# Joining chunk 4's scores to the sums of values: one group of four banks in a fused attention and expert kernel

## The chip, the cores and the metric

The kernel runs on one core of a Trainium2 chip. The time is the device time of one execution in microseconds (us). The kernel before took 1122.79 us in the median of three runs (1121.68, 1122.79 and 1124.22).

## What is computed

The reference is block-causal attention followed by a two-layer expert with a sigmoid gate, all in float32:

```python
batch, n_heads, seq, head_dim = (8, 8, 576, 64)
scores = scale * np.matmul(q, k.transpose(0, 1, 3, 2))
scores = np.where(block_i >= block_j, scores, -1000000000.0)   # blocks of 64
attn = np.exp(scores - np.max(scores, axis=-1, keepdims=True))
attn = attn / (np.sum(attn, axis=-1, keepdims=True) + 1e-09)
x = np.matmul(attn, v)            # to (4608, 512), heads side by side
...
h = x @ w_in                      # 512 to 2048
g = h * (1.0 / (1.0 + np.exp(-1.702 * h)))
return g @ w_out                  # 2048 to 512
```

## The kernel before

**Turns.** Heads go in pairs, 32 pairs, one pair a turn (`step(n)`, n from 0). The 576 queries of a head are cut into five chunks: chunk 0 has 64 queries, chunks 1 to 4 have 128, and chunk i sees 64 (2i + 1) keys, so chunk 4 sees all 576. The two heads of a pair lie on partitions 0 to 63 and 64 to 127, and their score matmuls (64 partitions each) run side by side on TensorE. An order of a turn is written out by hand in `ORDER`: each word is a slot, `3+0/2+1` scores chunks 3 and 0 in one pair of banks and 2 and 1 in another, `4` chunk 4, `V` the sums of values of the pair before (`av(n - 1)`), `L` the transposes of the next pair's queries and keys (`prep`). Between the slots the expert's matmuls are let in.

**Scores (`score`, `weigh`, `normalise`, `turn`).** For each chunk TensorE writes the scores into PSUM banks, `bank`. The vector engine adds the mask, scales and takes the row minimum in one instruction (L351, with an accumulator read for the maximum `mx`), ScalarE takes the exponential with a row sum (L358), the vector engine makes a scalar of the sum (L368, L371), and GpSimd (L376) or the vector engine (L378) scales the rows, as `SCALE_ON` says: "P" GpSimd, "D" the vector engine. From the ninth turn on (n of 8 and more) the vector engine turns the weights in 32x32 blocks (L385, L390), and behind chunk 4 sixteen DMAs on SP's queue put the blocks into their places (`turned<-turned`), where the next turn's sums of values read them. Before that TensorE turns them (`flip`). The tile of weights `e` has two buffers, one for chunks 0, 2 and 4, one for 1 and 3. Chunk 4's 576 keys do not fit a bank of 512: its scores are cut at 256, and take four banks.

**Banks.** `bank()` hands out tiles in a fixed round; from the tenth turn on there are four, w0 to w3. A tile can be written when the one before it in the same bank has been read.

**The expert.** Tokens go in 12 tiles of 384, the hidden layer in 16 chunks of 128 per tile. A hidden chunk is 12 matmuls into `hp` (one bank), then tanh on ScalarE (L562), the product `g` on the vector engine (L563), a high part `gh` on ScalarE (L571) and a low part `gl` on GpSimd (L82); the second layer is 9 matmuls into `acc` for the hidden chunk before. `hp` of the next hidden chunk can begin when `g` of this one has read the bank. So TensorE's list from the tenth turn on is a row of hp and acc, with a group of attention matmuls behind some hp. Six or so hidden chunks pass in a turn.

**What sets the order.** TensorE's matmuls stay in the order in which the program writes them (`keep_in_program_order`); on the other engines a scheduler at build time places the instructions, from the program's order and priorities (`tc.high_priority` for tanh, g, gh, gl and the tiles' splits xh and xl). Each engine then works off its list in order, and an instruction that waits holds up all behind it.

Of the kernel before, what the change touches and what calls it, by code (L numbers as in the profile page):

```python
# [10 lines left out]
F32 = mybir.dt.float32  # L11
# [5 lines left out]

SCALE_ON = ("PPPPP", "PPPPP", "PPPPD")  # L20

# [4 lines left out]
ORDER = (  # L26
# [3 lines left out]
)  # L30

START = "1+0 - B 2/3 L C - V - 4 - a - - -"
# [8 lines left out]
def attention_moe_kernel(  # L41
# [9 lines left out]
    nc = tc.nc  # L51
# [52 lines left out]

    ident = sp.tile([P, P], F32, name="ident")
    make_identity(nc, ident)
    MW = 448
    mask = sp.tile([P, MW], mybir.dt.bfloat16, name="mask")
    nc.gpsimd.memset(mask, 0.0)
    nc.gpsimd.memset(mask[0:BLK, MW - BLK : MW], -8e9)  # L110
# [16 lines left out]
        return home[name, g]  # L127

    xr = sp.tile([P, NDC, RING], F32, name="xr")


    vp = sp.tile([P, 2, NCH, D], F32, name="vp")
# [159 lines left out]
    def prep(n):  # L292

        tag = "e0" if early(n) and n % 2 else "qk"
        qk[n] = d2.tile([P, 2, S], F32, tag=tag, name="qk", bufs=1)
        for x in range(2):
            nc.vector.transpose(out=qk[n][:, x], in_=raw[n][:, x].rearrange("p c d -> p (c d)"))  # L297
        raw.pop(n)
        m = follower(n)
        if m is not None:  # L300
            load(m)

    stats = {}

    def score(n, banks):

        if n not in stats:
            mx = d2.tile([P, NCH + 1, 2], F32, tag="mx", name="mx")
            sm = d2.tile([P, NCH, 2], F32, tag="sm", name="sm")
            stats[n] = (mx, sm)  # L310
        todo = []
        for chunks in banks:

            part = []
            for lo, hi in ((0, 512),) if width(chunks[0]) <= 512 else ((0, 256), (256, S)):
                ss = [bank() for _ in range(2)]
                c = 0
                for i in chunks:
                    a, z = qrange(i)
                    w = min(hi, width(i)) - lo  # L320
                    for hd in range(2):
                        r = slice(hd * D, hd * D + D)

                        mm(
                            out=ss[hd][:, c : c + w], lhsT=qk[n][r, 0, a : a + P],
                            rhs=qk[n][r, 1, lo : lo + w], start=True, stop=True,
                        )
                        part.append((i, hd, lo, lo + w, ss[hd][0 : z - a, c : c + w]))
                    c += w
            todo.append(sorted(part, key=lambda x: (chunks[::-1].index(x[0]), x[2])))  # L330
        for chunks, part in zip(banks, todo):
            e = {}
            for i, hd, lo, hi, s in part:
# [30 lines left out]
    def normalise(n, i, e):  # L364
        _, sm = stats[n]
        m = BLK if i == 0 else P
        c = sm[0:m, i]
        nc.vector.tensor_scalar(  # L368
            out=c, in0=c, scalar1=1e-9, scalar2=2.0, op0=ALU.add, op1=ALU.mult
        )  # L370
        nc.vector.reciprocal(out=c, in_=c)  # L371
        on = SCALE_ON[phase(n)][i]
        for hd in range(2):
            x, sc = e[0:m, hd], c[:, hd : hd + 1]
            if on == "P":
                nc.gpsimd.tensor_tensor(out=x, in0=x, in1=sc.to_broadcast([m, width(i)]), op=ALU.mult)  # L376
            elif on == "D":
                nc.vector.tensor_scalar(out=x, in0=x, scalar1=sc, scalar2=None, op0=ALU.mult)  # L378
            else:
                nc.scalar.activation(out=x, in_=x, func=AF.Copy, scale=sc)  # L380

    def turn(n, i, e):

        for hd in range(2 if i else 0):
            nc.vector.transpose(  # L385
                out=tw[:, :, SLOT[i] : SLOT[i] + i, hd].rearrange("p b j c -> p j b c"),
                in_=e[:, hd, 0 : i * P],
            )
        r = slice(BLK, P) if i else slice(0, BLK)
        nc.vector.transpose(  # L390
            out=tw[r, 0:2, 9 + max(i, 1)].rearrange("p b h c -> p h b c"), in_=e[r, :, i * P : width(i)]
        )
        if i == NCH - 1:
            for kb in range(4):
                for qb in range(4):
                    ns = 10 if kb > 1 else NS if qb > 1 else 11
                    nc.sync.dma_start(
                        out=pw[kb * 32 : kb * 32 + 32, qb, 0:ns], in_=tw[qb * 32 : qb * 32 + 32, kb, 0:ns]
                    )
# [26 lines left out]
                in_=src[:, x : x + 2 * len(part), a : a + 2],  # L426
            )

    def av(n):

        b, h = divmod(n, HP)
        before_av(n)
        o, o0 = bank(), bank()

        todo = []
        for i in range(1, NCH):
            c = (i - 1) * P
            todo += [(o, c, P, j, pw[:, :, SLOT[i] + j]) for j in range(i)]
            todo.append((o, c + BLK, BLK, i, pw[:, 2:4, 9 + i]))
        last = len(todo) - 1  # L440
        todo.append((o0, 0, BLK, 0, pw[:, 0:2, 10]))

        for x, (bk, c, nn, j, w) in enumerate(todo):
            for hd in range(2):
                mm(
                    out=bk[hd * D : hd * D + D, c : c + nn].rearrange("d (a c) -> d a c", c=32),
                    lhsT=values(n)[:, hd, j], rhs=w[:, :, hd], start=x in (0, last + 1), stop=x >= last,
                )
# [12 lines left out]
    def order(n):  # L461
        return {HP: START, 2 * HP: HANDOVER}.get(n, ORDER[phase(n)]).split()

    def step(n):
# [112 lines left out]
        yield from second(prev)  # L577


    ends = np.cumsum([0.0] + [NFC * chunk_time(tt) for _, tt in TILES])  # L580

    def quota(pos):
        xs, ys = zip(*TILES_BY)
        return -1.0 if pos < xs[0] else np.interp(pos, xs, [ends[y if y >= 0 else y - 1] for y in ys])

    def heads_for(t):
        return -(-sum(TILES[t]) // S) * H
# [36 lines left out]
    for n in range(NPAIR + 1):  # L624
        items = step(n)
        for sl, fn in enumerate(items):
            if fn is not None:
                fn()
            if order(n)[sl] == "V":
# [35 lines left out]
```

## Time and profile before

| | |
|---|---|
| median of three runs | 1122.79 us |
| profiled execution, own time | 1120.49 us |
| its span, first to last instruction | 1118.6 us |
| mean granted TensorE clock | 0.992 of full speed |
| TensorE busy | 1076.4 us (96%) |
| vector engine busy (DVE) | 583.0 us (52%) |
| ScalarE busy (ACT) | 498.6 us (45%) |
| GpSimd busy (POOL) | 406.7 us (36%) |

The profile was taken by the hardware in one execution. A row of its timeline has the start and the duration in us, the engine, the line of the program, the operation, the tiles written and read (`out<-in`), the shape, a count where equal rows follow each other, and in brackets the idle time before it with what ended it. Matmuls are pipelined, and the duration of one reaches past the start of the next: what a matmul costs is read from start to start. A float32 matmul shows as two rows.

### The profile page before, as it was taken

The page shows a single profiled execution, that of the slowest core. Times are in us where ns is not written, and L with a number is a line of the kernel's source. Part 1 is how long each engine was busy: PE and PEld are TensorE (multiplying, and loading weights), DVE is VectorE, ACT ScalarE, POOL GpSimd, SP SyncE. Part 2 cuts the span into 40 slices and gives each one's busy share as a digit, 9 for nine tenths or more (in the row PEclk, how much of TensorE's full clock was granted, in tenths as well). Part 3 has the DMA queues.
Part 4 walks back from the last instruction along what each step waited for, and adds up shares of the span by engine and source line. Part 5 has one row for each costly group of instructions (what it writes and reads, how often), then busy time and mean ns, then how long its engine had stood idle before and what let it go on. Part 6 is the DMA issues. An engine that isn't in the chain of part 4 may idle for free. (4 is left out here: it accounts for less than half of the span.)

```text
span 1118.6 us, 19977 instructions
## 1 busy us (share of the span) xinstructions
PE 1076.4 (96%) x6960; PEld 908.7 (81%) x6960; DVE 583.0 (52%) x1856; ACT 498.6 (45%) x1321; POOL 406.7 (36%) x509
## 2 busy tenths in 40 slices
PE   5969998999999999999999999999999999999998
PEld 3757776788888888888888888888888888899997
DVE  6776885545545555654555655645545654211210
ACT  5866776434534433534443543444434444322322
POOL 4665664333333332333333333333333233122222
PEclk9979999999999999999999999999999999999999
DMA  8734532332444432343443333344342332200000
GB/s 171 205 89 153 150 73 62 84 79 57 105 86 86 103 80 64 64 98 78 98 101 74 75 93 65 70 108 85 81 107 63 71 85 58 54 29 1 29 1 29
DMA packets 219365, 91.25 MB, mean 82 GB/s; under 512 B 197760, under 2 KB 197760, under 8 KB 219264
## 3 DMA queue, kind: packets, MB, share of 16 engines
q1 hardware_dynamic: 214528, 89.38, 34.0%
q10 hardware_dynamic: 4736, 0.59, 0.3%
q8 instruction: 55, 0.90, 0.3%
q14 instruction: 46, 0.38, 0.1%
HBM read 45.09 MB, written 9.44 MB: 49 GB/s over the span
## 5 line engine op out<-in xcount | busy, mean ns | idle before, releaser
L82 POOL TENSOR_TENSOR gl<-g,gh 128x384 fp32r<-128x384 f32 x192 | 194.7, 1014 | 551.5 <-ACT gh L571 449.1
L99 PE MATMUL hp<-xh,wih 128*128 128x384 f32 x768 | 264.7, 345 | 7.9 <-DVE g L563 6.9
L563 DVE SCALAR_TENSOR_TENSOR g<-g,hp 128x384 f32<-128x384 f32 x192 | 105.9, 552 | 319.1 <-ACT g L562 317.8
L99 PE MATMUL hp<-xh,wil 128*128 128x384 f32 x768 | 258.4, 336 | 0.1
L562 ACT ACTIVATE g<-hp 128x384 f32<-128x384 f32 x192 | 94.1, 490 | 359.8 <-PE hp L99 354.8
L99 PE MATMUL hp<-xl,wih 128*128 128x384 f32 x768 | 253.9, 338 | 0.4 <-DVE xl L82 0.4
L99 PE MATMUL acc<-woh,gh 128*128 128x512 f32 x576 | 233.9, 406 | 0.0
L99 PE MATMUL acc<-wol,gh 128*128 128x512 f32 x576 | 226.9, 394 | 0.0
L99 PEld LDWEIGHTS hp<-xh,wih 128*128 128x128 f32 x768 | 144.2, 188 | 34.1 <-DVE g L563 23.1
L99 PE MATMUL acc<-woh,gl 128*128 128x512 f32 x576 | 167.9, 393 | 0.3 <-POOL gl L82 0.3
L571 ACT CAST gh<-g 128x384 fp32r<-128x384 f32 x192 | 98.4, 513 | 156.5 <-DVE g L563 156.4
L99 PEld LDWEIGHTS hp<-xh,wil 128*128 128x128 f32 x768 | 144.3, 188 | 6.5 <-POOL wil L82 0.7
L358 ACT ACTIVATE e<-e,mx 64x64 f32<-64x64 f32 (+4 forms) x240 | 132.3, 552 | 37.6 <-DVE mx L351 37.6
L376 POOL TENSOR_TENSOR e<-e,sm 64x64 f32<-64x64 f32 (+1 forms) x192 | 113.6, 612 | 95.0 <-DVE sm L371 46.5
L99 PEld LDWEIGHTS hp<-xl,wih 128*128 128x128 f32 x768 | 143.6, 188 | 1.3 <-DVE xl L82 1.3
L99 PE MATMUL bank<-qk 64*128 64x320 f32 (+4 forms) x768 | 122.5, 428 | 14.5 <-DVE qk L297 11.1
L99 PEld LDWEIGHTS acc<-woh,gh 128*128 128x128 f32 x576 | 107.9, 187 | 34.2 <-issue 10.5
L99 PEld LDWEIGHTS acc<-woh,gl 128*128 128x128 f32 x576 | 107.8, 188 | 25.9 <-POOL gl L82 1.2
L99 PEld LDWEIGHTS acc<-wol,gh 128*128 128x128 f32 x576 | 108.3, 188 | 16.7 <-POOL wol L82 0.3
L351 DVE CUSTOM_DVE_ANT_0 e<-bank,mask 64x64 f32<-64x64 f32 (+4 forms) x240 | 89.7, 417 | 56.9 <-PE bank L99 52.8
L385 DVE STREAM_TRANSPOSE turned<-e 128x384 f32<-128x384 f32 (+1 forms) x192 | 92.3, 499 | 48.8 <-POOL e L376 48.3
L99 PEld LDWEIGHTS bank<-qk 64*128 64x128 f32 x768 | 69.6, 193 | 54.2 <-issue 25.4
(50 smaller groups left out, 956.0 us busy)
## 6 DMA issues: line engine op xcount, KB each, us to landing
turned<-turned SPq DMA_DIRECT2D x192, 80.0 KB, 2.1
turned<-turned SPq DMA_DIRECT2D x96, 112.0 KB, 2.2
raw<-in_q_dram SPq DMA_DIRECT2D x128, 72.0 KB, 2.4
out_dram<-osb SPq DMA_DIRECT2D x36, 256.0 KB, 2.2
raw<-in_k_dram SPq DMA_DIRECT2D x120, 72.0 KB, 2.6
turned<-turned SPq DMA_DIRECT2D x96, 88.0 KB, 2.1
words<-in_moe_w_in_dram SPq DMA_DIRECT2D x16, 512.0 KB, 6.3
vp<-in_v_dram SPq DMA_DIRECT2D x60, 128.0 KB, 2.4
```

Of the source, the lines that this page charges most:

```text
L82: eng.tensor_tensor(out=out, in0=in0, in1=in1, op=ALU.subtract)
L99: return tc.keep_in_program_order(nc.tensor.matmul(**kw))
L351: nc.vector.tensor_tensor_reduce(out=e[0:m, hd, lo:hi], in0=s, in1=mk, op0=ALU.add, op1=ALU.min, scale=-0.125, scalar=3e38 if lo == 0 else ...
L358: nc.scalar.activation(out=e[0:m, hd], in_=e[0:m, hd], func=AF.Exp, scale=-1.0, bias=mx[0:m, i, hd : hd + 1], accum_out=sm[0:m, i, hd : hd ...
L376: nc.gpsimd.tensor_tensor(out=x, in0=x, in1=sc.to_broadcast([m, width(i)]), op=ALU.mult)
L385: nc.vector.transpose(out=tw[:, :, SLOT[i] : SLOT[i] + i, hd].rearrange("p b j c -> p j b c"), in_=e[:, hd, 0 : i * P],)
L562: nc.scalar.activation(out=g, in_=hp[:, 0:tt], func=AF.Tanh, scale=1.702)
L563: nc.vector.scalar_tensor_tensor(out=g, in0=g, scalar=1.0, in1=hp[:, 0:tt], op0=ALU.add, op1=ALU.mult)
L571: nc.scalar.copy(out=gh, in_=g)
```

## The change

From the tenth turn on (n of 9 and more) the slot `V4` takes the place of `V` and `4`. It takes a bank `o0`, runs the sums of values of the pair before, and scores chunk 4 of this pair directly behind. Chunk 4's first 512 keys of each head go into a bank of their own; the last 64 keys of both heads are one matmul of 128 partitions against a tile `ends`, in which the two heads' keys stand on the diagonal with zeros beside them, and their scores lie in the unused part of `o0`. So the group takes four banks, o0, o and two more, in place of two and then four. `V4` stands in the ninth place of thirteen, where `V` was in the fifth and `4` in the eighth. The last 64 keys are transposed into `ends` by two small instructions in `prep`. Chunk 4's scaling from the ninth turn on is "M": GpSimd takes the first head, the vector engine the second; the transposes of all chunks are written with the second head first. In the sums of values the matmuls of block 0 come first, in place of last. The mask has 576 columns in place of 448.

```diff
-SCALE_ON = ("PPPPP", "PPPPP", "PPPPD")
+SCALE_ON = ("PPPPP", "PPPPP", "PPPPM")
...
-    "3+0/2+1 - - - V - - 4 - - - L -",
+    "3+0/2+1 - - - - - - - V4 - - L -",
...
-    MW = 448
+    MW = 576
...
+    ends = sp.tile([P, 2, BLK], F32, name="ends")
+    nc.gpsimd.memset(ends, 0.0)
...
-            nc.vector.transpose(out=qk[n][:, x], in_=raw[n][:, x].rearrange("p c d -> p (c d)"))
+            z = QC * P if x and n > 2 * HP else S
+            nc.vector.transpose(out=qk[n][:, x, 0:z], in_=raw[n][:, x, 0 : z // 32].rearrange("p c d -> p (c d)"))
+            for hd in range(2 if z < S else 0):
+                r = slice(hd * D, hd * D + D)
+                nc.vector.transpose(
+                    out=ends[r, hd], in_=raw[n][r, x, z // 32 : S // 32].rearrange("p c d -> p (c d)")
+                )
...
-    def score(n, banks):
+    def score(n, banks, shared=None):
...
-            for lo, hi in ((0, 512),) if width(chunks[0]) <= 512 else ((0, 256), (256, S)):
+            cuts = (0, 512) if width(chunks[0]) <= 512 or shared is not None else (0, 256, S)
+            for lo, hi in zip(cuts, cuts[1:]):
...
+            if shared is not None:
+                i = NCH - 1
+                mm(
+                    out=shared, lhsT=qk[n][:, 0, slice(*qrange(i))], rhs=ends.rearrange("p h k -> p (h k)"),
+                    start=True, stop=True,
+                )
+                part += [(i, hd, QC * P, S, shared[:, hd * BLK : (hd + 1) * BLK]) for hd in range(2)]
...
-            if on == "P":
+            if on == "P" or on == "M" and hd == 0:
...
-            elif on == "D":
+            elif on != "A":
...
-        for hd in range(2 if i else 0):
+        for hd in (1, 0) if i else ():
...
-    def av(n):
+    def av(n, o0=None):
...
-        o, o0 = bank(), bank()
+        o = bank()
+        if o0 is None:
+            o0 = bank()
...
+        todo.insert(0, (o0, 0, BLK, 0, pw[:, 0:2, 10]))
         last = len(todo) - 1
-        todo.append((o0, 0, BLK, 0, pw[:, 0:2, 10]))
...
+    def values_and_4(n):
+        o0 = bank()
+        av(n - 1, o0)
+        if n < NPAIR:
+            score(n, [[NCH - 1]], o0[:, BLK : 3 * BLK])
...
+            if x == "V4":
+                return lambda: values_and_4(n)
```

The instructions move as follows in the 19th turn. First TensorE, before; hp_5472 and hp_5568 are hidden chunks of the expert's first layer, acc0 is the second layer, bank_5492 the sums of values, bank_5588 and bank_5592 chunk 4:

```order
L99 MATMUL hp_5472<-xl_978,wih_1123 128x384
L99 MATMUL bank_5492<-turned_75,vp_73 64x128 x8
L99 MATMUL acc0_4979<-woh_1335,gh_5457 128x512
...
L99 MATMUL hp_5568<-xl_978,wih_1123 128x384
L99 MATMUL bank_5588<-qk_5333 128x256
L99 MATMUL bank_5592<-qk_5333 128x320
L99 MATMUL acc0_4979<-woh_1335,gh_5553 128x512
```

The sums stand behind one hidden chunk, chunk 4 behind a later one, each followed by the second layer. TensorE at the same place now; bank_5545 takes block 0's sums and then the scores against `ends`:

```order
L99 MATMUL hp_5525<-xl_980,wih_1125 128x384
L99 MATMUL bank_5545<-turned_77,vp_75 64x64 x2
L99 MATMUL bank_5546<-turned_77,vp_75 64x128 x8
...
L99 MATMUL bank_5583<-qk_5326 128x512
L99 MATMUL bank_5584<-qk_5326 128x512
L99 MATMUL bank_5545<-ends_73,qk_5326 128x128
L99 MATMUL acc0_4973<-woh_1337,gh_5510 128x512
```

Chunk 4's scores have moved up to the sums, with block 0's sums at the start of the group and the matmul against `ends` at its end.

The vector engine around chunk 4, before; e_5415 is chunk 2, e_5596 chunk 4, qk_5655 the next pair's queries and keys, g_5648 belongs to the first hidden chunk behind chunk 4's scores:

```order
L390 STREAM_TRANSPOSE turned_75<-e_5415 64x2x2x32
L563 SCALAR_TENSOR_TENSOR g_5552<-g_5552,hp_5539 128x384
L351 ISA e_5596,mx_5374<-bank_5588,mask_69 128x256
L563 SCALAR_TENSOR_TENSOR g_5581<-g_5581,hp_5568 128x384
...
L297 STREAM_TRANSPOSE qk_5655<-raw_5336 128x576 x2
L378 TENSOR_SCALAR e_5596<-e_5596,sm_5375 128x576 x2
L385 STREAM_TRANSPOSE turned_75<-e_5596 128x4x4x32 x2
L563 SCALAR_TENSOR_TENSOR g_5648<-g_5648,hp_5635 128x384
```

Between chunk 2's transpose and the first part of chunk 4's reduction stands a g, and a second g between its two parts. The vector engine at the same place now; g_5538 is of the hidden chunk just ahead of the group, e_5388 is chunk 3, e_5405 and e_5410 are chunks 1 and 2, e_5588 is chunk 4, g_5640 and g_5683 are of hidden chunks behind the group:

```order
L591 SCALAR_TENSOR_TENSOR g_5538<-g_5538,hp_5525 128x384
L403 STREAM_TRANSPOSE turned_77<-e_5388 128x3x4x32 x2
L369 ISA e_5405,mx_5369<-bank_5377,mask_69 128x192
...
L408 STREAM_TRANSPOSE turned_77<-e_5410 64x2x2x32
L369 ISA e_5588,mx_5369<-bank_5583,mask_69 128x512
...
L396 TENSOR_SCALAR e_5588<-e_5588,sm_5370 128x576
L403 STREAM_TRANSPOSE turned_77<-e_5588 128x4x4x32
L591 SCALAR_TENSOR_TENSOR g_5640<-g_5640,hp_5627 128x384
...
L591 SCALAR_TENSOR_TENSOR g_5683<-g_5683,hp_5670 128x384
L302 STREAM_TRANSPOSE qk_5647<-raw_5331 128x512
```

From chunk 3's transposes to chunk 4's, no g is left in the list, and the transpose of the next pair's keys has moved from ahead of chunk 4's scaling to behind a later g.

On ScalarE the copy of block 0's sums (`xr<-bank`, L450 before) comes ahead of the copy of the others.

More of the change, by code (lines that the diff above doesn't have):

```diff
@@ L446, in av @@
                     out=bk[hd * D : hd * D + D, c : c + nn].rearrange("d (a c) -> d a c", c=32),
-                    lhsT=values(n)[:, hd, j], rhs=w[:, :, hd], start=x in (0, last + 1), stop=x >= last,
+                    lhsT=values(n)[:, hd, j], rhs=w[:, :, hd], start=x in (0, 1), stop=x in (0, last),
                 )
@@ L577, in moe @@
         yield from second(prev)
-    ends = np.cumsum([0.0] + [NFC * chunk_time(tt) for _, tt in TILES])
+    tile_ends = np.cumsum([0.0] + [NFC * chunk_time(tt) for _, tt in TILES])
     def quota(pos):
         xs, ys = zip(*TILES_BY)
-        return -1.0 if pos < xs[0] else np.interp(pos, xs, [ends[y if y >= 0 else y - 1] for y in ys])
+        return -1.0 if pos < xs[0] else np.interp(pos, xs, [tile_ends[y if y >= 0 else y - 1] for y in ys])
     def heads_for(t):
@@ L628, in attention_moe_kernel @@
                 fn()
-            if order(n)[sl] == "V":
+            if order(n)[sl][0] == "V":
                 heads_done = 2 * n
```

## The prediction

> **What bounds the kernel now.** I read the page first, then the table by stretches, then the timelines of TensorE and of the vector engine over one turn. Columns of a stretch: busy time of each engine, TensorE's granted clock, DMA share, GB/s.
>
> ```profile
> PE 1076.4 (96%) x6960; PEld 908.7 (81%) x6960; DVE 583.0 (52%) x1856; ACT 498.6 (45%) x1321; POOL 406.7 (36%) x509
> 220.00:960.00 740.00, 734.62 (x4807) 623.86 (x4804) 403.78 (x1340) 309.43 (x836) 247.60 (x321) 1.00 0.37 83
> ```
>
> From 220 us on, where the changed turns lie, TensorE is busy for 734.6 of 740 us: what it loses there is added to the end, what it doesn't do is taken off. The other engines have half their time free, so their busy sums decide nothing; their order does, since each works off its list in order. These TensorE rows are from one turn (262.95: the sums of values; 270.23: chunk 4), two from a later turn, the last two from the stretch after attention:
>
> ```profile
> 262.95 2.99 PE L99 MATMUL bank<-turned,vp 128*64 128x128 f32 x60
> 265.86 0.50 PE L99 MATMUL acc<-woh,gh 128*128 128x512 f32 x1
> 270.23 1.24 PE L99 MATMUL bank<-qk 64*128 64x256 f32 x8
> 273.58 0.33 PE L99 MATMUL hp<-xh,wih 128*128 128x384 f32 x1
> 275.69 0.39 PE L99 MATMUL acc<-woh,gh 128*128 128x512 f32 x1
> 278.78 0.45 PE L99 MATMUL hp<-xh,wih 128*128 128x384 f32 x1 [0.85 <-DVE g L563]
> 758.19 0.39 PE L99 MATMUL acc<-woh,gh 128*128 128x512 f32 x1
> 760.44 0.45 PE L99 MATMUL hp<-xh,wih 128*128 128x384 f32 x1
> 984.64 0.39 PE L99 MATMUL acc<-woh,gh 128*128 128x512 f32 x1
> 986.72 0.33 PE L99 MATMUL hp<-xh,wih 128*128 128x384 f32 x1
> ```
>
> The acc group takes 2.08 undisturbed (984.64 to 986.72), hp 2.11 (273.58 to 275.69). At 275.69 it took 3.09: the next hp waited 1.01 us for the vector engine's g, because hp has one bank. At 758.19 it took 2.25: a wait of 0.17. The vector engine in the turn at 262.95 shows why, and carries most of what follows:
>
> ```profile
> 263.63 0.56 DVE L563 SCALAR_TENSOR_TENSOR g<-g,hp 128x384 f32<-128x384 f32 x1 [3.64 <-ACT g L562]
> 264.11 1.03 DVE L385 STREAM_TRANSPOSE turned<-e 128x384 f32<-128x384 f32 x2
> 265.28 0.36 DVE L351 CUSTOM_DVE_ANT_0 e<-bank,mask 128x192 f32<-128x192 f32 x1
> 266.66 0.08 DVE L351 DVE_READ_ACCUMULATOR2_ANT mx<- 128x1 f32 x1
> 266.70 0.17 DVE L368 TENSOR_SCALAR sm<-sm 128x2 f32<-128x2 f32 x1
> 271.32 0.31 DVE L390 STREAM_TRANSPOSE turned<-e 64x128 f32<-64x128 f32 x1
> 271.77 0.43 DVE L351 CUSTOM_DVE_ANT_0 e<-bank,mask 128x256 f32<-128x256 f32 x1
> 272.12 0.55 DVE L563 SCALAR_TENSOR_TENSOR g<-g,hp 128x384 f32<-128x384 f32 x1
> 273.40 0.55 DVE L351 CUSTOM_DVE_ANT_0 e<-bank,mask,mx 128x320 f32<-128x320 f32 x1
> 273.87 1.44 DVE L297 STREAM_TRANSPOSE qk<-raw 128x576 f32<-128x576 f32 x2
> 275.24 0.17 DVE L368 TENSOR_SCALAR sm<-sm 128x2 f32<-128x2 f32 x1
> 275.64 0.95 DVE L378 TENSOR_SCALAR e<-e,sm 128x576 f32<-128x576 f32 x2
> 276.51 1.30 DVE L385 STREAM_TRANSPOSE turned<-e 128x512 f32<-128x512 f32 x2
> 278.17 0.55 DVE L563 SCALAR_TENSOR_TENSOR g<-g,hp 128x384 f32<-128x384 f32 x1
> ```
>
> Chunks 2 and 1 take 6.35 us (265.28 to 271.63). Chunk 4 takes 6.40 more, to the g at 278.17; its scores (270.23) waited until 271.77 for this engine. The tiles e of chunks 2 and 4 share one buffer (`e{i % 2}`), so this sequence can't be swapped.
>
> **The change: TensorE's own work.** In the 23 turns with n from 9 to 31 the two groups become one; by the lists of TensorE in the section on the change, two hidden chunks that stood between the sums and chunk 4 now stand ahead of them. Prices:
>
> ```profile
> 752.47 0.34 PE L99 MATMUL hp<-xl,wih 128*128 128x384 f32 x1
> 752.74 1.24 PE L99 MATMUL bank<-qk 64*128 64x256 f32 x8
> 753.91 0.50 PE L99 MATMUL acc<-woh,gh 128*128 128x512 f32 x1
> 754.25 0.39 PE L99 MATMUL acc<-wol,gh 128*128 128x512 f32 x1
> 754.47 0.39 PE L99 MATMUL acc<-woh,gh 128*128 128x512 f32 x1
> 90.12 0.82 PE L102 MATMUL bank<-ident,turned 128*128 128x128 f32 x6
> 90.69 0.48 PE L99 MATMUL acc<-woh,gh 128*128 128x512 f32 x1
> ```
>
> Entering the group takes 0.27 (752.47 to 752.74) where hp steps take 0.17 in the same timeline (2.11 over 12): 0.10 lost. Behind it the first acc takes 0.34 (753.91 to 754.25), the next 0.22: 0.11 lost. So chunk 4 costs 0.10 + 1.17 + 0.11 = 1.38 now, and the acc behind the sums loses 0.11 as well. In one group stand two 64x512 that run side by side, 0.95 (1.17 less 0.10 for leaving, times 512 of 576 columns), 0.10 to change the array's shape, and the ends, whose 128 rows find no partner: six 128x128 passes took 0.57 at 90.12, this one has two, and with some loss at the start I take 0.28. [...] That is 1.33 for 1.38 + 0.11, a gain of 0.16 a turn, **4 us** in 23 turns; with the ends at nothing or at twice the price it is 10 us or a loss of 3. The old g waits fall away too: 1.01 and about 0.1 for a slow restart (0.45 in place of 0.33) in six turns of the pattern above, and some 0.4 in the other 17, which wait twice, 0.17 and less, and restart twice: 6 x 1.1 + 17 x 0.4 = **13 us** gained.
>
> **What is late next.** By the lists of the vector engine in the section on the change, chunks 2 and 1 still begin behind the g of the hidden chunk that ends where the sums begin, as at 263.63, but chunk 4's scores follow with nothing of the expert between, and the next g stands behind chunk 4's scaling and transpose. Three waits come of it; time 0 is the start of the sums (262.95 in the rows).
>
> *Banks.* Four banks go round, so chunk 4's 64x512 take the two that chunks 2 and 1 leave. The last maximum is read out at 3.79 (266.74), and TensorE, done with the sums at 2.92, starts at about 3.85: **0.93**. This order, g and both transposes ahead of the reduces, stands in 9 of the 23 turns; in two more a mixed one costs half; in 12 the reduces begin a microsecond earlier or more, and the banks come in time. Sum 9 us.
>
> *The g behind chunk 4.* Chunk 4's reduces start where 271.77 lies: 8.82. Four of them take 1.6 (2.10 from 271.77 to 273.87, less the 0.48 of a g that stands among them). The sums' scalars come 1.84 after the first head's last reduce (273.40 to 275.24), here, where that is the third of four and done 0.2 before their end, at 1.4 + 1.84 = 3.24; reciprocal 0.40; one head's scaling 0.44 and its transpose 0.66: g at 8.82 + 4.74 = 13.56, and hp 0.61 behind (278.17 to 278.78): 14.17. TensorE would be there at 3.85 + 0.95 + 0.10 + 0.28 and acc, hp, acc (2.16 + 2.11 + 2.08) = 11.53. So **2.6**. I went through the 23 turns in the same way: 6 like this, 6 whose reduces begin directly behind the g, with the banks in time (2.3), 2 with both transposes and the small one ahead of the g (3.9), 8 others from 1.6 to 2.7, and turn 9 with none. 6 x 2.6 + 6 x 2.3 + 2 x 3.9 + 8 x 2.3 = **56 us**.
>
> *Keys.* In 12 turns the transpose of the next pair's keys (qk_5647, 128x512) stands behind the g of the hidden chunk that is the last before those scores. That g starts 0.68 after TensorE would begin them (263.63 less 262.95), then 0.48, 0.65 for the transpose, 0.06 to TensorE: **1.85**. Before, both key transposes were through by 275.31 (273.87 + 1.44). 12 x 1.85 and a microsecond for three tile starts: 23 us.
>
> The other parts: GpSimd's half of the scaling is hidden where the g stands between the transposes. A 128x448 there takes 0.93, so 128x576 about 1.13 (0.93 + 128 x 0.0016, the step from 0.72 for 128x320), done before the second transpose is wanted; in four turns both transposes precede the g, which is in the 3.9 above.
>
> ```profile
> L376 POOL TENSOR_TENSOR e<-e,sm 128x448 f32<-128x448 f32 x34 | 31.0, 933 | 9.5 <-DVE sm L371 9.5
> L376 POOL TENSOR_TENSOR e<-e,sm 128x320 f32<-128x320 f32 x34 | 23.8, 720 | 20.6 <-DVE sm L371 20.6
> ```
>
> [...] The two small transposes into `ends` (a 64x128 one took 0.31) replace part of the key transpose and stand where the engine waits anyway. The 16 DMAs that turn e are issued some 2 us later behind the scores than now, and are read a turn later, some 20 us on; the loads of values and keys that stand behind them on SP's queue have as long. The longer mask and `ends` are set before the first maxima. The scheduler also shuffles some vector and GpSimd steps in the first nine turns, where TensorE idles anyway: -4 to +4.
>
> Sum on the profiled execution (span 1118.6, own time 1120.5, 2.3 under the median of the runs, 1122.8): 1120.5 + 9 + 56 + 23 - 13 - 4 = 1191.5; on the median's scale **1194**.
>
> **Rivals.** *The clock falls.* The waits of 2.5 and more are long enough to ask what TensorE's clock does:
>
> ```profile
> 0.00:28.00 28.00, 16.18 (x82) 10.45 (x84) 18.77 (x72) 16.57 (x50) 13.59 (x29) 0.94 0.87 171
> 56.00:75.00 19.00, 12.55 (x80) 9.05 (x80) 14.98 (x42) 13.91 (x41) 11.76 (x15) 0.64 0.51 130
> 58.69 0.76 PE L99 MATMUL bank<-qk 64*128 64x192 f32 x8 [2.52 <-DVE qk L297]
> 160.00:220.00 60.00, 54.02 (x368) 42.31 (x366) 35.67 (x108) 31.82 (x84) 26.19 (x31) 1.00 0.27 68
> 188.30 1.20 PE L102 MATMUL bank<-ident,turned 128*128 128x128 f32 x9 [2.00 <-POOL turned L376]
> ```
>
> An idle 2.5, with more idle time behind it, went with a clock of 0.64, an idle 2.0 with 1.00. One short drop cost 0.06 x 28 = 1.7 us in the first stretch. If half of some 16 long waits pay that, 14 us come on top: 1208. [...]
>
> *A shorter chain.* In the chain from 266.70 to 271.32 the vector engine mostly waits for GpSimd. If TensorE's new idle time lets that work come earlier by one microsecond, the g waits fall by 22 and the banks' by half: 1167.
>
> *Faster.* Chunk 4's scaling and the g get through before the next hp: it decides if the g can start by 10.9 in place of 13.56, as it would were chunks 2 and 1 worked off before the sums begin. Then the 4 and 13 us are gained and no wait is new: 1106. For it speaks that turn 9 has that order; against it, the order of 22 others.
>
> **How the numbers follow.** Sum as above 0.60 (own range 1177 to 1211), clock 0.22, shorter chain 0.14, faster 0.04. The range leaves out the last and some of the edges: 1165 to 1220. A difference under 0.2%, 2 us, couldn't be told from none: faster 0.04, same 0.01, slower 0.95.
>
> **What would show it.** Right: hp rows that wait 2 to 3 us for g after chunk 4, bank rows at qk 64x512 waiting for mx (about 1 us, 9 to 11 times), bank rows waiting for the key transposes 12 times at 1.8; a turn of some 37 us in place of 32; TensorE's busy sum unchanged. Wrong: hp following acc at 2.08 in most turns, or a clock well under 1.00 between 220 us and the end.

## The result and the profile after

The changed kernel takes 1249.81 us in the median of four runs (1247.80 to 1254.99) against 1123.51 before: ratio 1.113, 95% interval 1.111 to 1.116. Forecast were 1194 and a range to 1220. The profiled execution took 1249.79, its span is 1248.0, 129.4 more than before. One execution of a kernel told below, the one with the group in the sixth slot, took 2093.85 us at full clock; it is left out of that kernel's figures.

The two traces can be laid side by side at hidden chunks, which are the same 192 in both. I cut at the 19th, where the tenth turn is about to begin, and at the 157th, behind the last turn. Table by stretches, before and then after (length, busy TensorE, weight loads, vector engine, ScalarE, GpSimd, granted clock, DMA share, GB/s):

```profile
0.00:213.08 213.08, 180.23 (x1306) 139.94 (x1306) 152.71 (x468) 142.69 (x392) 120.33 (x150) 0.96 0.48 124
213.08:958.17 745.09, 739.71 (x4831) 627.94 (x4830) 406.19 (x1345) 310.46 (x839) 248.84 (x323) 1.00 0.37 83
958.17:1118.60 160.43, 156.42 (x826) 140.78 (x824) 24.09 (x44) 45.49 (x91) 37.49 (x37) 1.00 0.06 21
```

```profile
0.00:225.58 225.58, 189.23 (x1305) 148.16 (x1306) 153.99 (x469) 143.18 (x392) 121.39 (x152) 0.92 0.46 117
225.58:1087.86 862.28, 776.80 (x4785) 658.15 (x4784) 408.06 (x1366) 308.27 (x839) 281.78 (x347) 0.95 0.32 71
1087.86:1248.00 160.14, 156.32 (x826) 140.75 (x824) 24.18 (x44) 45.57 (x91) 36.79 (x37) 1.00 0.06 21
```

The middle stretch is 117.2 longer. Idle time of TensorE grew from 5.4 to 85.5 (862.28 less 776.80); the other 37 lie in busy time, which grew from 739.7 to 776.8 for nearly the same work, at a clock of 0.95 in place of 1.00. The first stretch is 12.5 longer, and its clock fell from 0.96 to 0.92. The waits of TensorE in the middle stretch, before and after (waited for, us in total, times, longest):

```profile
PE hp L99 <- DVE g L563: 5.1, 6, 0.9
```

```profile
PE hp L99 <- DVE g L591: 56.3, 23, 4.0
PE bank L99 <- DVE qk L302: 25.0, 12, 3.3
PE bank L99 <- DVE mx L369: 4.1, 9, 0.5
```

These are the three waits of the forecast, with its counts; two of the sums are nearly the forecast's, and the third row leaves a part out, of which below. One turn on TensorE, then the group alone in a turn where the banks come late:

```profile
608.69 2.98 PE L99 MATMUL bank<-turned,vp 128*64 128x64 f32 x60
611.61 1.13 PE L99 MATMUL bank<-qk 64*128 64x512 f32 x4
612.67 0.49 PE L99 MATMUL bank<-ends,qk 128*128 128x128 f32 x2
612.91 0.48 PE L99 MATMUL acc<-woh,gh 128*128 128x512 f32 x1
615.08 0.34 PE L99 MATMUL hp<-xh,wih 128*128 128x384 f32 x1
...
621.89 0.44 PE L99 MATMUL hp<-xh,wih 128*128 128x384 f32 x1 [2.46 <-DVE g L591]
622.17 0.33 PE L99 MATMUL hp<-xh,wil 128*128 128x384 f32 x1
...
622.59 0.52 PE L99 MATMUL hp<-xh,wih 128*128 128x384 f32 x1
622.91 0.52 PE L99 MATMUL hp<-xh,wil 128*128 128x384 f32 x1
...
627.61 2.11 PE L99 MATMUL bank<-qk 64*128 64x448 f32 x16 [1.94 <-DVE qk L302]
...
650.06 1.53 PE L99 MATMUL bank<-qk 64*128 64x512 f32 x4 [0.46 <-DVE mx L369]
651.52 0.49 PE L99 MATMUL bank<-ends,qk 128*128 128x128 f32 x2
```

Sums, chunk 4 and the matmul against `ends` run without a gap; the second hp behind them waits 2.46 for g, and from 622.59 on its matmuls follow each other by 0.32 in place of 0.17: half clock. At 650.06 the row shows a wait of 0.46, but that is the first head's matmul only: the second head's starts 0.41 behind it (0.01 at 611.61), just after the last maximum is read at 650.33, and the whole group takes 1.46 to the matmul against `ends` in place of 1.06 (611.61 to 612.67). So the bank wait is 0.86 there. The trace has nine such groups, and two more in which the second head alone waits its 0.40: 8.6 us, of which 4.4 count as busy. The vector engine in the turn of 608.69, and GpSimd's half of the scaling:

```profile
609.38 0.55 DVE L591 SCALAR_TENSOR_TENSOR g<-g,hp 128x384 f32<-128x384 f32 x1 [2.69 <-ACT g L590]
609.86 0.35 DVE L369 CUSTOM_DVE_ANT_0 e<-bank,mask 128x192 f32<-128x192 f32 x1
616.46 0.69 DVE L369 CUSTOM_DVE_ANT_0 e<-bank,mask 128x512 f32<-128x512 f32 x1
619.73 0.17 DVE L386 TENSOR_SCALAR sm<-sm 128x2 f32<-128x2 f32 x1 [0.86 <-ACT e L376]
620.13 0.52 DVE L396 TENSOR_SCALAR e<-e,sm 128x576 f32<-128x576 f32 x1
621.33 0.52 DVE L591 SCALAR_TENSOR_TENSOR g<-g,hp 128x384 f32<-128x384 f32 x1
626.29 0.55 DVE L591 SCALAR_TENSOR_TENSOR g<-g,hp 128x384 f32<-128x384 f32 x1 [3.22 <-ACT g L590]
626.76 0.70 DVE L302 STREAM_TRANSPOSE qk<-raw 128x512 f32<-128x512 f32 x1
```

```profile
620.24 1.41 POOL L394 TENSOR_TENSOR e<-e,sm 128x576 f32<-128x576 f32 x1 [4.73 <-DVE sm L389]
```

From 609.86 to 616.46 stand chunks 2 and 1 (6.6 us), then chunk 4 to its scaling, and only then the g that TensorE waits for; the key transpose stands behind the next g (626.76) and ends 0.15 ahead of the start of the scores that need it.

**The clock.** The record of the granted clock has nothing but 1.00 and 0.50, and the stretches of 0.50, 27 in this trace, are 3.41 us or a multiple of it (the last one, at 1247.1, ends with the trace) and start on one grid of that step. Stretches cut on this grid, around the turn above and around a turn with a longer wait (2.58) and no drop:

```profile
615.59:619.01 3.42, 3.42 (x19) 3.10 (x18) 3.12 (x11) 0.94 (x3) 0.00 (x0) 1.00 0.00 0
619.01:622.42 3.41, 0.95 (x5) 0.53 (x4) 2.58 (x6) 1.58 (x4) 1.41 (x1) 1.00 0.00 0
622.42:625.84 3.42, 3.25 (x11) 2.74 (x9) 0.58 (x3) 0.07 (x1) 1.01 (x1) 0.50 0.44 105
...
656.56:659.97 3.41, 1.71 (x8) 1.06 (x6) 2.44 (x11) 2.00 (x5) 0.77 (x1) 1.00 0.00 0
659.97:663.38 3.41, 2.38 (x12) 2.06 (x12) 1.99 (x5) 0.56 (x2) 1.67 (x2) 1.00 0.14 35
```

In the first turn the wait fell whole into one window, TensorE was busy 0.95 of 3.41, and the next window ran at half clock. In the second the grid cut the wait into 1.70 and 0.88, and nothing followed. I counted all full-speed windows behind 150 us in this trace and in those of all experiments but the last told: the 138 in which TensorE was busy for less than 0.44 of the window were all followed by half clock, of 22 between 0.44 and 0.48 nine were, of 3,868 above it three. So in these traces it was not the length of a wait that decided but what of it lay in one window: with over 1.9 us of it there (busy for less than 0.44), a window at half clock followed each time. In all the traces hp's matmuls follow each other by 0.320 there and by 0.174 at full clock (medians), so a half-clock window loses 46% of its busy time, 1.6 us if it is full of work.

### The profile page after: what moved, and what is told of

It reads as the page before. It is cut to its first block, busy times and chain, and to the rows that moved or that the text cites. A ratio compares the mean times of both kernels' runs of the same rounds, so it can differ in the third digit from the quotient of the medians.

```text
span 1248.0 us, 20061 instructions
## 1 busy us (share of the span) xinstructions
PE 1122.4 (90%) x6914; PEld 947.1 (76%) x6914; DVE 586.2 (47%) x1878; ACT 497.0 (40%) x1321; POOL 440.0 (35%) x534
## 4 chain that ended last, share of the span: by engine, by line
PE 55%; DVE 11%; ACT 6%; POOL 5%; issue 5%; DMA 1%; SPq 1%; DVEq 0%; POOLq 0%; ACTq 0%
PE hp L99 26%; PE acc L99 22%; PE bank L99 6%; POOL e L394 5%; ACT e L376 4%; DVE turned L403 3%; DVE e L369 2%; DVE g L591 1%; DVE turned L408 1%; ACT g L590 1%; DVE qk L302 1%; DVE sm L386 1%; DVE e L396 1%; DVE sm L389 1%; DMA turned<-turned 1%
## 5 line engine op out<-in xcount | busy, mean ns | idle before, releaser
L99 PE MATMUL hp<-xh,wih 128*128 128x384 f32 x768 | 272.0, 354 | 57.5 <-DVE g L591 57.4
L99 PE MATMUL hp<-xh,wil 128*128 128x384 f32 x768 | 268.3, 349 | 1.3 <-POOL wil L82 1.3
L99 PE MATMUL hp<-xl,wih 128*128 128x384 f32 x768 | 264.4, 351 | 0.4 <-DVE xl L82 0.4
L394 POOL TENSOR_TENSOR e<-e,sm 64x64 f32<-64x64 f32 (+4 forms) x216 | 147.2, 699 | 217.4 <-DVE sm L389 183.9
L99 PEld LDWEIGHTS hp<-xh,wih 128*128 128x128 f32 x768 | 150.3, 196 | 79.8 <-DVE g L591 68.3
L99 PE MATMUL bank<-qk 64*128 64x320 f32 (+5 forms) x676 | 134.9, 492 | 41.4 <-DVE qk L302 32.6
L99 PEld LDWEIGHTS hp<-xh,wil 128*128 128x128 f32 x768 | 150.6, 196 | 8.9 <-POOL wil L82 2.1
L99 PEld LDWEIGHTS hp<-xl,wih 128*128 128x128 f32 x768 | 151.0, 197 | 1.2 <-DVE xl L82 1.2
L369 DVE CUSTOM_DVE_ANT_0 e<-bank,mask 64x64 f32<-64x64 f32 (+5 forms) x240 | 100.7, 468 | 30.3 <-PE bank L99 24.5
```

The lines of the kernel that those rows point to most:

```text
L99: return tc.keep_in_program_order(nc.tensor.matmul(**kw))
L369: nc.vector.tensor_tensor_reduce(out=e[0:m, hd, lo:hi], in0=s, in1=mk, op0=ALU.add, op1=ALU.min, scale=-0.125, scalar=3e38 if lo == 0 else ...
```

## The experiments

For every kernel I took the stretch from the 19th hidden chunk to the 157th: its length; the idle time in it; the half-clock windows in it and what they cost (46% of TensorE's busy time inside them); and the rest, TensorE's work at full speed. In the changed kernel, with the scaling alone and with block 0 last the rest holds 4.4 us of bank waits of the second head, with the keys first 8.5; in the other joined kernels 1.2 or less.

| kernel | median us | ratio (95%) | stretch | idle | windows, cost | rest |
|---|---|---|---|---|---|---|
| before | 1123.5 | | 745.1 | 5.4 | 0 | 739.7 |
| after | 1249.8 | 1.111-1.116 | 862.3 | 85.5 | 24, 34.4 | 742.4 |
| before, one long wait a turn | 1211.1 | 1.076-1.080 | 832.7 | 64.9 | 16, 24.6 | 743.1 |
| before, two short waits | 1187.7 | 1.054-1.060 | 806.5 | 57.8 | 2, 3.1 | 745.6 |
| after, taken apart | 1141.9 | 1.015-1.019 | 755.2 | 13.0 | 0 | 742.2 |
| after, own buffer late | 1183.2 | 1.052-1.056 | 793.5 | 47.2 | 5, 7.8 | 738.5 |
| after, shared tile | 1162.9 | 1.035-1.038 | 780.4 | 33.2 | 6, 9.3 | 737.8 |
| after, keys first | 1258.9 | 1.119-1.124 | 873.7 | 90.0 | 26, 37.5 | 746.2 |
| after, shared tile, keys first | 1161.2 | 1.032-1.036 | 781.5 | 35.9 | 7, 8.9 | 736.7 |
| after, three repairs | 1181.3 | 1.048-1.053 | 806.3 | 53.9 | 11, 14.9 | 737.4 |
| after, scaling alone | 1245.4 | 1.106-1.111 | 855.3 | 79.3 | 24, 34.1 | 741.9 |
| after, block 0 last | 1245.4 | 1.106-1.110 | 866.9 | 85.9 | 26, 38.5 | 742.6 |
| after, shared tile, slot 6 | 1140.7 | 1.013-1.017 | 762.4 | 19.9 | 3, 4.7 | 737.8 |
| after, shared tile, slot 7 | 1128.8 | 1.003-1.006 | 752.7 | 12.9 | 1, 1.6 | 738.2 |
| before, shared tile | 1134.9 | 1.007-1.013 | 758.2 | 13.6 | 4, 6.0 | 738.7 |
| before, shared tile late | 1120.7 | 0.998-1.000 | 742.6 | 5.4 | 0 | 737.2 |

### The clock: one long wait or two short ones

The same idle time was put into the kernel before, at one place of a turn or at two:

```diff
+                    k = t * NFC + fc
+                    for _ in range(7 if 24 <= k < 150 and k % 6 in (0,) else 0):
+                        nc.scalar.copy(out=g, in_=g)
```

> The kernel before, with seven copies of g onto itself on ScalarE ahead of the product of every sixth hidden chunk from the 25th to the 150th: 21 times one artificial wait of TensorE of about 2.8 us, nothing else changed. Theory (the clock is set for windows of 3.41 us on a fixed grid, and a window in which TensorE was busy for less than about 0.45 is followed by one at half clock): 12 to 18 half-clock windows between 220 us and the end, 59 us of waits and 20 to 27 of clock: 1204 us. [...]

The second kernel has `range(4 ...)` and `k % 6 in (0, 4)`:

> As the run with one artificial wait, but the idle time is split: four copies ahead of the product at two places of a turn, 42 waits of about 1.4 us, 59 us in sum. Theory (windows of 3.41 us with a limit at about 0.45 busy, that is 1.9 us idle): no half-clock window, 1182 us. Rival (the clock goes by the share of idle time over a longer stretch): as many half-clock windows as with one long wait, 1204 us.

Waits of TensorE in the stretch, one long wait and then two short ones:

```profile
PE hp L99 <- DVE g L566: 64.8, 26, 4.0
```

```profile
PE hp L99 <- DVE g L566: 57.3, 42, 2.5
```

16 half-clock windows and 24.6 us against 2 and 3.1 for nearly the same idle time: the reading by windows holds, and the second run's rival falls (a share over a longer stretch would give as many in both). Length alone doesn't explain it either: in the first only two waits, of 4.01, are longer than a step of 3.41, and most are 2.2 to 3.0. The second kernel was to have no such window; its two stand behind two of its four waits of 2.4, which were not intended, and of the 32 waits of 1.3 to 1.8 none cost one. Both kernels took 6 to 7 us more than expected (1204 and 1182). A part of that is slow restarts, to which I had given no price: the second has 36 waits more than the kernel before and 5.9 us more work (745.6 less 739.7), the first 20 and 3.4, some 0.16 for each wait.

### The place: the group taken apart

```diff
-    "3+0/2+1 - - - - - - - V4 - - L -",
+    "3+0/2+1 - - - V - - 4s - - - L -",
...
+            if x == "4s":
+                return (lambda: score(n, [[NCH - 1]], bank()[:, BLK : 3 * BLK])) if now else None
```

> The changed kernel with the group taken apart again: the sums of values in the fifth slot, chunk 4 in the eighth, as before the change; the cut at 512 keys, the tile ends, GpSimd's half of the scaling and the order of the sums stay. Theory (the place of chunk 4's scores, directly behind the sums, costs nearly all, through the vector engine's order and TensorE's clock): no g wait over 1 us and no key wait from the tenth turn on, no half-clock window there; what was lost ahead of the tenth turn (12.5 us) stays: 1132 us, 1122 to 1140. Rival (the parts themselves cost: three banks, two more small transposes, GpSimd and the vector engine side by side): 1180 us or more.

With the cut at 512, `ends` and the shared scaling in place, but the sums in the fifth slot and chunk 4 in the eighth, the long waits of the changed kernel are gone (13.0 of g waits in 23, none over 1.2) and so are the half-clock windows. 108 of the 126 us are the place. This kernel came out 2 us above its expected range, with five waits of 1.1 to 1.2 where none over 1 was expected. The parts themselves cost the rest: by the profiled executions 2.5 in TensorE's work (742.2), 7.6 in small g waits and 9.8 ahead of the tenth turn.

### What makes the g late

Theory: chunks 2 and 1 stand ahead of chunk 4 because chunk 1 waits for chunk 3's buffer. First a buffer of its own, which is free only from n = 16 on:

```diff
-            e = d2.tile([P, 2, w], F32, tag=f"e{i % 2}", name="e", bufs=1)
+            e = d2.tile([P, 2, w], F32, tag="wm" if i == 1 and n > 15 else f"e{i % 2}", name="e", bufs=1)
```

> The changed kernel, with a buffer of its own for chunk 1's weights from n = 16 on, so that chunks 1 and 2 can be reduced and scaled well before the sums of values, and only transposes stand between the g ahead of the group and chunk 4's reduction. Theory (the 6.35 us of chunks 2 and 1 ahead of chunk 4 make the g late): in the 16 turns from n = 16 on the g waits of 2.6 us go, the bank waits too; the key waits stay (some ten of 1.9 us) with a half-clock window behind every second; 52 us less than the changed kernel, 1197 us, 1180 to 1212. Rival (chunk 4's own chain of reduction, exponential, scaling on two engines and transposes is the cost): within 15 us of the changed kernel.

Then chunks 1 and 2 in one tile, from n = 8 on:

```diff
+            if i in (1, 2):
+                if n not in pair12:
+                    pair12[n] = d2.tile([P, 2, 512], F32, tag="e0", name="e12", bufs=1)
+                e = pair12[n][:, :, 0:192] if i == 1 else pair12[n][:, :, 192:512]
+            else:
+                e = d2.tile([P, 2, w], F32, tag=f"e{i % 2}", name="e", bufs=1)
```

> The changed kernel with chunks 1 and 2 side by side in one tile (192 and 320 of 512 keys) in the buffer of chunks 0, 2 and 4, from the ninth turn on: chunk 1 need no longer wait until chunk 3 has left its buffer, and in the vector engine's list both stand long ahead of the sums, so that only six transposes lie between the g ahead of the group and chunk 4's reduction. Theory (the 6.35 us of chunks 2 and 1 made the g late): no g wait over 1 us and no bank wait in the 23 turns, the key waits stay (25 us, some 5 half-clock windows): 1160 us, 1148 to 1172. Rival (chunk 4's own chain makes the g late): g waits of over 1.5 us stay, 1200 us or more.

Waits, own buffer late and then shared tile:

```profile
PE bank L99 <- DVE qk L302: 25.4, 12, 3.3
PE hp L99 <- DVE g L591: 20.4, 21, 4.1
PE bank L99 <- DVE mx L369: 1.4, 3, 0.5
```

```profile
PE bank L99 <- DVE qk L302: 24.1, 12, 2.3
PE hp L99 <- DVE g L597: 9.0, 21, 1.3
```

The buffer that helps from n = 16 on takes two thirds of the g waits (1183.2 us, in the expected range), the tile takes them from 56.3 to 9.0, the bank waits to nothing, the key waits stay to the count of 12: as expected, in time too (1162.9 for 1160), but for two g waits of 1.2 and 1.3. A vector engine row of the shared tile, in the turn whose sums begin at 639.45, shows it: chunk 4's reduction waits for TensorE there, where in the changed kernel TensorE waited for it.

```profile
640.61 1.15 DVE L409 STREAM_TRANSPOSE turned<-e 128x128 f32<-128x128 f32 x4
643.53 0.69 DVE L375 CUSTOM_DVE_ANT_0 e<-bank,mask 128x512 f32<-128x512 f32 x1 [1.76 <-PE bank L99]
```

### Moving the key transposes

```diff
+    def prep_first(n):
+        with tc.high_priority(offset=600 if n > 9 else 0):
+            prep(n)
```

> The changed kernel, with a higher priority for the transposes of the next pair's queries and keys from the tenth turn on: on the vector engine all four stand between the two parts of chunk 4's reduction, none behind a g. Theory (three waits of one engine's order, each its own): the 12 key waits (25.0 us) go, the g waits grow by the transposes that now stand ahead of them (0.7 + 0.5 less the 0.66 of chunk 4's transpose that the g now precedes, some 0.6 in 22 waits, 13 us), and some 6 half-clock windows fewer: 1230 us, 1215 to 1245. Rival (the key waits only stand where TensorE would wait for the same chain anyway): no change, 1245 to 1255.

> Both edits together, the shared tile of chunks 1 and 2 and the priority of the key transposes. Theory: from the tenth turn on no wait over 1.2 us and no half-clock window; TensorE's own work there 738 us, waits 5 to 12 us; the loss ahead of the tenth turn (12 us) stays: 1133 us, 1124 to 1145, so that the join by itself is worth no more than the few us of the switches. Rival (something else of the change costs TensorE's time): over 1150 us.

Waits, keys first and then keys first with the shared tile:

```profile
PE hp L99 <- DVE g L595: 77.8, 22, 4.0
PE bank L99 <- DVE mx L373: 11.1, 21, 1.1
```

```profile
PE hp L99 <- DVE g L601: 35.9, 24, 5.0
```

Both expectations on the sum were wrong (1258.9 for 1230, 1161.2 for 1133). The key waits go in both, but the g and bank waits take their place, 28.5 more in the first and 26.9 in the second: the transposes now stand between TensorE and the g, and the scheduler, with other priorities, puts steps of chunks 2 and 1 behind the g again. A third try wrote the transposes between chunk 4's reduction and its scaling, with the shared tile and block 0 last outside the group:

```diff
+            if shared is not None and n + 1 < NPAIR:
+                prep(n + 1)
             for i in chunks[::-1]:
                 normalise(n, i, e[i])
```

> The join with three repairs: the shared tile of chunks 1 and 2; the transposes of the next pair's queries and keys written between chunk 4's reduction and its scaling, where the vector engine waits for ScalarE's exponential; block 0's sums last again where the sums stand alone (up to the ninth turn). Theory: no key wait; the g behind chunk 4 (through at about 10.9 us from the start of the sums, and hp 0.06 behind it, where TensorE comes at 10.6) waits 0.3 to 0.6 us in most of 23 turns, 10 to 16 us with two or three longer waits where the tile's split stands among chunk 4's steps; no or few half-clock windows; TensorE's own work from the tenth turn on 737 us; ahead of it 214 us: 1130 us, 1120 to 1140. Rival (the join gains its 4 us and more once its waits are gone): under 1120 us.

It missed by 51: g waits of 52.7 (24 waits, 12 of them 1.9, the longest 5.5). The transposes of chunks 3, 1 and 2 stand behind a wait for GpSimd there, so chunk 4's reduction begins late again. My reading of the list had given this wait no price.

### The place again, with the shared tile

The group in the sixth and in the seventh slot, with two hidden chunks or one more between it and the next scores; both kernels have the shared tile, and block 0's sums last where the sums stand alone. The order of the seventh:

```diff
-    "3+0/2+1 - - - - - - - V4 - - L -",
+    "3+0/2+1 - - - - - V4 - - - - L -",
```

> The join with the shared tile of chunks 1 and 2, block 0's sums last where the sums stand alone, and the joined group in the sixth slot of thirteen in place of the ninth: between it and the next scores lie two hidden chunks more, so that the key transposes have left before the last g. Theory (the three waits are a matter of place and order, the join itself gains the switches): no key wait, no bank wait, g waits of 0.3 to 0.5 us in most of 23 turns (10 us), one or two half-clock windows at most; TensorE's own work from the tenth turn on 737 us, 747 us in all; ahead of it 215 to 219 us: 1126 us, 1119 to 1133. Rival (the joined group carries a cost of its own wherever it stands): 1140 us or more.

> As the run with the joined group in the sixth slot, with the group in the seventh: one hidden chunk fewer behind it. Theory: the same within 5 us, since in every turn at least one g still stands behind the key transposes; 1127 us, 1119 to 1135. Rival (the place alone decides, and each slot later costs a part of what the ninth costs): 5 to 15 us more than in the sixth.

Waits in the sixth and then in the seventh slot, and the vector engine ahead of the longest wait of the seventh (at 265.32, 3.20):

```profile
PE hp L99 <- DVE g L599: 19.2, 25, 3.4
```

```profile
PE hp L99 <- DVE g L599: 12.2, 27, 3.2
```

```profile
264.37 0.31 DVE L414 STREAM_TRANSPOSE turned<-e 64x128 f32<-64x128 f32 x1 [1.57 <-POOL e L400]
264.71 0.56 DVE L599 SCALAR_TENSOR_TENSOR g<-g,hp 128x384 f32<-128x384 f32 x1
```

No key wait and no bank wait in either. The seventh slot is 0.5% slower than the kernel before (0.3 to 0.6%), 5 of the 126 us, so the join carries no large cost of its own. I had expected both kernels within 5 us of each other; they lie 12 apart. The sixth came out at the rival's time, but not by the rival's cause: four waits of 2.7 to 3.4 in turns n = 10 to 16, of which the seventh has one, in which a g stands behind a small transpose that waits for GpSimd, take 12.5 of its 19.9, and its half-clock windows follow them. The cost doesn't grow slot by slot.

### The smaller parts

Chunk 4's scaling on the vector engine alone (`"PPPPD"`), and block 0's sums last where the sums stand alone:

> The changed kernel with chunk 4's scaling on the vector engine alone, as before the change. Theory (the two halves run side by side, and the g in the list stands behind two scalings and no transpose in place of one scaling and one transpose, 0.95 for 1.15): the g waits shrink by 0.2 each, some 5 us, and the clock does what it will: 1245 us, 1235 to 1255. Rival (GpSimd and the vector engine hold each other up in the two halves, and that makes the g late): 1225 us or less.

> The changed kernel, with block 0's sums last again where the sums stand alone (turns up to n = 8), first only in the joined group. Theory (in the ninth turn the first sum waits for the bank that the last maximum leaves, 4.3 us in place of 1.5, and a half-clock window follows): the start of the 19th hidden chunk comes at 216 to 221 us in place of 225.6, and the whole is 5 to 9 us faster than the changed kernel: 1242 us, 1236 to 1248. Rival (the first nine turns lose their time to the scheduler's shuffle alone): within 3 us of the changed kernel.

Both medians came out 4.4 us lower. For the first that isn't clear of the scatter (1242.3 and 1248.5 in two runs, from 1247.8 on in the changed kernel), but its g waits shrink as the list says, from 56.3 to 50.4. In the changed kernel the two halves run side by side, the vector engine's in 0.52 (0.95 for two before) and GpSimd's in 1.40; the 16 rows of GpSimd with 128x576 in the earlier turns took 1.15, where I had put 1.13. Beside the vector engine, and starting 0.11 later, GpSimd's half thus took 0.25 longer than those; what lengthens it was not shown. The second edit brings the 19th hidden chunk from 225.6 to 217.5, as expected. The row with block 0's sums in the ninth turn, before, after and with the edit:

```profile
199.44 0.34 PE L99 MATMUL bank<-turned,vp 128*64 128x64 f32 x4 [1.52 <-DVE mx L351]
```

```profile
207.33 5.60 PE L99 MATMUL bank<-turned,vp 128*64 128x64 f32 x60 [4.32 <-DVE mx L369]
```

```profile
203.93 0.34 PE L99 MATMUL bank<-turned,vp 128*64 128x64 f32 x4 [1.53 <-DVE mx L369]
```

Block 0's bank is the one that the last maximum leaves. Put first, it holds up all 60 matmuls; put last, only itself. The rest of the 8 us was lost again to two half-clock windows more.

### The shared tile without the join

> The kernel before with the shared tile of chunks 1 and 2 alone. Theory (the old g waits, 5.4 us of idle time and about as much in slow restarts, came of the same order on the vector engine): 1117 us, 1112 to 1122. Rival (the old waits have another cause, or the edit only moves them): 1122 to 1126.

Slower, by 1.0%, outside what theory and rival allowed: four waits of 2.7 to 3.4, again a g behind a transpose that waits for GpSimd, in turns n = 10 to 15, and four half-clock windows. The later turns were faster by some 0.2 us each, so the last kernel has the tile only there (`and n > 15`):

> The kernel before with the shared tile of chunks 1 and 2 from n = 16 on alone. In the run with it from the ninth turn on, the later turns lost 0.79 us each beside TensorE's plain hp and acc, 0.94 to 1.1 in the kernel before, and four of the earlier ones lost 3.4 to 3.6 us to a g that stands behind transposes that wait for GpSimd. Theory (both readings hold, the early turns stay as before): 15 times 0.2, 3 us less than the kernel before: 1120 us, ratio 0.996 to 0.999. Rival (the few tenths of waits in the later turns are given back elsewhere): the same as before, within 0.1%.

1120.7, ratio 0.9987 (0.9977 to 0.9997): it beats the kernel before by 0.13%, half of what I expected, and the interval reaches into the rival's 0.1%. No joined kernel beats the kernel before.

## Why the prediction was wrong

The direction, the mechanism and the three waits were right; the time was 56 us too low. On the profiled executions 1191.5 were forecast and 1249.8 measured: of these 58 us the clock is 34, the first nine turns 12.5, gains that did not come 10, the waits 2.

**The three waits.** "*The g behind chunk 4.* ... 56 us": 56.3, and not by luck: in the turn whose sums begin at 646.61, g stands at 13.67 and hp at 14.24 from there, forecast were 13.56 and 14.17. "*Keys.* ... 12 turns ... 23 us": 25.0, in 12 (the four terms of one wait add to 1.87, not 1.85). "*Banks.* ... 9 us": 8.6, nine waits of 0.86 where I had 0.93, and two of half that. 88 forecast, 89.8 measured.

**The gains.** "13 us" for the old g waits and "4 us" for the switches, 17 in all. The stretch after, less its waits (89.8) and the clock's 34.4, is 738.1, so 7 less than the 745.1 before. The forecast charged old waits with a slow restart and the new ones with none: 38 waits more at the 0.16 of the two runs with artificial waits are 6 us. Of the other 4, 2 are the first acc behind the matmul against `ends`, which the forecast let begin without a loss. No run shows that: its step to the next matmul took 0.32 in the 23 turns (median; 612.91 to 613.23 in the turn above), where behind hp it takes 0.23. The rest is open, and no run measures the switches alone.

**The step that failed** is "*The clock falls.* ... If half of some 16 long waits pay that, 14 us come on top", which I left out of the sum and gave a chance of 0.22. It costs 34.4 us in the middle stretch, and the sign that was to show the forecast wrong, a clock well under 1.00 behind 220 us, is there: 0.95. The price of one drop (1.7) was nearly right, 1.6 for a full window and 1.4 in the mean; the number was not: 24 windows for 8. I had two rows, an idle 2.5 with a drop and an idle 2.0 without, and looked for a limit in length between them; that the sum could do without a term for the clock was my estimate, and no run shows it. The trace of before held a hint of the better reading: its half-clock stretches are 3.41 and 13.65 long, one and four steps of a grid. The limit of 1.9 was found only behind the result. With windows, an estimate from the step of 3.41 and the limit of 1.9: a wait of length L drops the clock with the chance that over 1.9 of it lie in one: (3.41 - L + 2(L - 1.9)) / 3.41 (and 1 from 3.41 on), 0.60 for the 23 g waits of 2.45 in the mean and 0.5 for the 12 key waits of 2.1, 20 drops. The trace has 20, of which three lasted two or three windows: 24. Worked out wait by wait, the formula gives 19 here, and 108 for the 113 drops in the same stretch of the other 13 traces, the same ones from which the limit was read.

**The first nine turns.** "The scheduler also shuffles some vector and GpSimd steps ... -4 to +4": 12.5. 8.1 of it is block 0's place in the sums (217.5 against 225.6), an edit of the diff that I had named only for its copy on ScalarE: it moves a bank's wait from the last two matmuls to the first of all, 2.8 us, and half-clock windows follow. What makes the other 4.4 is open; up to 3 of it may be scatter, since three kernels whose edits lie behind the 19th hidden chunk (one long wait, two short waits, shared tile late) reach it at 214.8 to 216.2, the kernel before at 213.1.

**Rivals.** "*A shorter chain*" and "*Faster*" both rested on work of chunks 2 and 1 being done earlier. The runs with the shared tile show that this does take the g waits away (56.3 to 9.0), and that the key waits then remain, which "Faster" had overlooked: 1163, not 1106. With the key waits gone as well, in the seventh slot, it is 1128.8, still 0.5% above the kernel before.

## What to carry to other kernels

Where the clock goes by windows, as here, price a wait twice: its length, and one window at half clock times the chance that enough of it falls into one window; the same idle time in short pieces is cheaper (here the half-clock windows cost 25 us with one long wait a turn and 3 with two short ones). Before two groups are joined on the busiest engine, look at what its helper has between their two results: a stretch that used to be covered by work in between is laid bare. A step that is only moved within the helper's list gives its time back elsewhere; what helps is to free the buffer that keeps it from being done early.

## What was not expected of the hardware

In these traces the limit of the clock's window lies near 0.44 to 0.48 of busy time (all of 138 windows below it were followed by half clock, three of 3,868 above it), so waits of 1.9 to 2.6 already cost, and whether one does is a matter of where the grid lies; in the run with three repairs, ten of the 12 waits of 1.9 left the clock alone. A half-clock window that is itself not full is followed by another: of all those behind 150 us, the 25 that were busy for less than 0.79 were (two of them at 192.3 and 776.0 in the changed kernel), of eight between 0.79 and 0.85 five, of 148 fuller ones none.
